# An adaLN, linear attention and SwiGLU block: shift and scale from eight row blocks of w_mod, and row tile 3 turned by a DMA

## The chip, the cores and the metric

The kernel runs on one core of a Trainium2 chip. The metric is the device time of one launch in microseconds. Eleven runs of the kernel before gave a median of 839.13 us (836.94 to 840.78).

## The reference

x is 2048 rows of 1024 features in bf16. A condition vector c gives six vectors of 1024: shift, scale and gate for the attention (sa, ca, ga) and for the feed-forward part (sb, cb, gb).

```
mod = silu(c) @ w_mod                      # 1024 x 6144 -> sa, ca, ga, sb, cb, gb
h = layernorm(x) * (1 + ca) + sa
q, k, v = split(h @ wqkv)                  # 32 heads of 32
pq, pk = phi(q), phi(k)                    # phi(t) = (t + 1 if t > 0 else exp(t)) + 1e-6
o = (pq @ (pk^T v)) / (pq @ sum(pk) + 1e-6)
x = x + ga * (o @ wo)
h = layernorm(x) * (1 + cb) + sb
x = x + gb * ((silu(h @ w_gate) * (h @ w_up)) @ w_down)
```

## The kernel before

The 2048 rows are four chunks of 512 (`sc`), each four row tiles of 128 (`t`). A normalised chunk is kept turned, features on partitions: `hT` is 128 partitions x 8 feature blocks (`cc`) x 512 rows. Shift and scale are then one value per partition and feature block, and `modulate` (line 217, instruction at 218) is one VectorE (DVE) operation for each `cc`. For every chunk come the keys (`k_mms`, 279: a group is one row tile and half of the columns, 8 matmuls over `cc`; eight groups, 64 matmuls), the values (`v_phase`, 297), and for the first chunk the queries; later the attention output and the feed-forward part follow.

This change is about the opening, up to the first value matmul. Both halves of `w_mod` that the attention needs (shift, columns 0 to 1023; scale, columns 1024 to 2047) are loaded here. Before, the view `wm_v` gives partition p the eight rows 8p to 8p + 7, and each tile `wme[b][q]` holds 512 columns of one of the two vectors, so rows of 1 KB are moved (`load_mod`, 130). SyncE's queue (SP) issues the loads in the order written in lines 123 to 149: x tiles 0 to 2, c, the first half of scale and of shift, key weights `wk` blocks 0 and 1 (`load_k`, 133), x tile 3, and so on; then the value weights `wv` (two tiles of 1 MB), x tiles 4 to 7 and the query weights `wq`.

`mod_block` (253) makes the columns of shift and scale: for each block of 128 columns eight matmuls with `w_mod` as stationary operand and the one column `scT` as moving one, so the result already lies on partitions. The layer norm of a tile is `ln1_stats` (231: two `bn_stats`, one aggregation on DVE, the power on GpSimd, POOL) and `ln1_norm` (238: ScalarE, ACT, or DVE for tile 3). In the first chunk TensorE turns the tiles (`pe_transpose_tile`, 221), and ACT and DVE share the copies out of PSUM. In later chunks a DMA turns them (`dma_start_transpose`, 245).

The order is written out by hand. `mm` and `transpose` (97 to 101) keep TensorE in program order, and the block `with in_order(...)` (424) does so for DVE, ACT and POOL. In it stand, on TensorE: tiles 0 to 2 turned, scale and shift of feature blocks 0 to 3, the first six key groups (row tiles 0 to 2) for `cc` 0 to 2, tile 3 turned, `cc` 3, then the second half's modulation between the rest. `keep_warm` (413) puts in filler matmuls whose result nobody reads: 20 at the start, 5 later. The tile framework gives each load from SP and ACT one of eight completion counters in turn; a load that takes a counter again waits until the load which used it last has landed.

Of the kernel before, what the change touches and what calls it, by code (L numbers as in the profile page):

```python
# [8 lines left out]
ACT = mybir.ActivationFunctionType  # L9
ALU = mybir.AluOpType  # L10
BF16 = mybir.dt.bfloat16
F32 = mybir.dt.float32
# [9 lines left out]
def kernel(  # L22
# [13 lines left out]
    nc = tc.nc  # L36
    P = nc.NUM_PARTITIONS
    _, S, D = A_x.shape
# [4 lines left out]
    DC = D // P  # L43
    HG = DC
    FC = F // P
    SCW = 512
    NSC = S // SCW
    STC = SCW // P
    NB = 512
# [13 lines left out]
    wg_v = B_w_gate.rearrange("(c p) f -> p c f", p=P)  # L63
    wu_v = B_w_up.rearrange("(c p) f -> p c f", p=P)
    wd_v = B_w_down.rearrange("(f p) n -> p f n", p=P)
    wm_v = w_mod.rearrange("(p j) n -> p j n", j=DC)
    c_v = c.rearrange("o (p j) -> p (o j)", j=DC)

    const = ctx.enter_context(tc.tile_pool(name="const", bufs=1))
    dram = ctx.enter_context(tc.tile_pool(name="dram", bufs=1, space=DRAM))  # L70
# [3 lines left out]
    ep = ctx.enter_context(tc.tile_pool(name="ep", bufs=3))  # L74
# [5 lines left out]
    last_on = {}  # L80
# [16 lines left out]
    def mm(out, lhsT, rhs, start, stop):  # L97
        return tc.keep_in_program_order(nc.tensor.matmul(out, lhsT=lhsT, rhs=rhs, start=start, stop=stop))  # L98

    def transpose(out, in_):  # L100
        return tc.keep_in_program_order(nc.tensor.transpose(out, in_, ident[:]))  # L101

    def big(name, shape):
        return k8.tile([P] + shape, BF16, name=name, tag="k8")
# [4 lines left out]
    def acc_b(name, shape=(NB,), dt=F32):  # L109
        return pb.tile([P] + list(shape), dt, name=name, tag="pb")  # L110

    x1_dram = dram.tile([S, D], F32, name="x1_scratch")

    c_sb = const.tile([P, DC], BF16, name="c_sb")

    x_tiles = {}

    def load_x(st, eng):
        x_sb = k2.tile([P, D], BF16, name="x_sb")
        eng.dma_start(out=x_sb[:], in_=x2[st * P:(st + 1) * P, :])  # L120
        x_tiles[st] = x_sb

    for st in range(STC - 1):
        load_x(st, nc.sync)
    nc.sync.dma_start(out=c_sb[:], in_=c_v)  # L125

    wk = [big("wk", [4, D]), big("wk", [4, D])]
    wme = [[big("wme", [DC, NB]) for _ in range(2)] for _ in range(2)]

    def load_mod(b, q, lo, hi):  # L130
        nc.sync.dma_start(out=wme[b][q][:, :, lo:hi], in_=wm_v[:, :, q * D + b * NB + lo:q * D + b * NB + hi])  # L131

    def load_k(cc):
        nc.sync.dma_start(out=wk[cc // 4][:, cc % 4, :], in_=wqkv_v[:, cc, D:2 * D])

    load_mod(0, 1, 0, NB)
    load_mod(0, 0, 0, NB)
    load_k(0)
    load_k(1)
    load_x(STC - 1, nc.sync)  # L140
    load_k(2)
    load_k(3)
    load_mod(1, 1, 0, NB)
    load_mod(1, 0, 0, NB // 2)
    load_k(4)
    load_k(5)
    load_mod(1, 0, NB // 2, NB)
    load_k(6)
    load_k(7)

    def load_w(view, lo, name):
        ts = []
# [11 lines left out]
    ident = const.tile([P, P], BF16, name="ident")  # L164
    make_identity(nc, ident[:])
    neg_half = const.tile([P, 1], F32, name="neg_half")
    nc.vector.memset(neg_half[:], -0.5)

    scT = const.tile([P, DC], BF16, name="scT")
    sc32 = const.tile([P, DC, 32], BF16, name="sc32")  # L170

    saT = const.tile([P, DC], F32, name="saT")
    ca1T = const.tile([P, DC], F32, name="ca1T")
    sbT = const.tile([P, DC], F32, name="sbT")
    cb1T = const.tile([P, DC], F32, name="cb1T")
    ga_t = ep.tile([P, NB], F32, name="e")
# [25 lines left out]
    def bn(src, mv_out):  # L202
        stats = small.tile([P, NNB, nc.vector.BN_STATS_DIM], F32, name="stats")
        for i in range(NNB):
            nc.vector.bn_stats(out=stats[:, i, :], in_=src[:, i * NB:(i + 1) * NB])
        nc.vector.bn_aggr(out=mv_out, in_=stats[:])

    def normalise(dst, src, mean, rstd):
        nc.vector.tensor_scalar(out=dst, in0=src, scalar1=mean, scalar2=rstd, op0=ALU.subtract, op1=ALU.mult)
# [7 lines left out]
    def modulate(hT, cc, scaleT, biasT, lo=0, hi=SCW):  # L217
        nc.vector.tensor_scalar(out=hT[:, cc, lo:hi], in0=hT[:, cc, lo:hi], scalar1=scaleT[:, cc:cc + 1],  # L218
                                scalar2=biasT[:, cc:cc + 1], op0=ALU.mult, op1=ALU.add)

    def pe_transpose_tile(hT, xn, t, split):
        tp = acc_b("tp", (DC, P), BF16)
        for cc in range(DC):
            transpose(tp[:, cc, :], xn[:, cc * P:(cc + 1) * P])
        if split < DC:
            nc.scalar.copy(out=hT[:, split:DC, t * P:(t + 1) * P], in_=tp[:, split:DC, :])
        nc.vector.tensor_copy(out=hT[:, 0:split, t * P:(t + 1) * P], in_=tp[:, 0:split, :])

    hTs = {}

    def ln1_stats(sc, t):
        x_sb = x_tiles.pop(sc * STC + t)
        mv = small.tile([P, STC, 2], F32, name="mv")
        bn(x_sb, mv[:, 0, :])
        rstd = rstd_of(mv, 1)
        return sc, t, x_sb, mv, rstd

    def ln1_norm(sc, t, x_sb, mv, rstd, dve=False):
        xn = k2.tile([P, D], BF16, name="xn", bufs=4)
        if dve:  # L240
            normalise(xn[:], x_sb[:], mv[:, 0, 0:1], rstd[:, 0:1])
        else:
            normalise_act(xn[:], x_sb[:], mv, rstd)
        if sc > 0:
            nc.sync.dma_start_transpose(hTs[sc][:, :, t * P:(t + 1) * P], xn[:])
        return xn
# [3 lines left out]
        for t in range(STC):  # L250
            ln1_norm(*ln1_stats(sc, t))

    def mod_block(b, q, lo, hi):
        for i in range(lo, hi):
            col = q * DC + 4 * b + i
            for j in range(DC):
                mm(mod_ps[:, col:col + 1], lhsT=wme[b][q][:, j, i * P:(i + 1) * P],
                   rhs=scT[:, j:j + 1], start=(j == 0), stop=(j == DC - 1))
        cs = slice(4 * b + lo, 4 * b + hi)
        src = mod_ps[:, q * DC + 4 * b + lo:q * DC + 4 * b + hi]  # L260
        if q == 1:
            nc.vector.tensor_scalar_add(out=ca1T[:, cs], in0=src, scalar1=1.0)
        else:
            nc.vector.tensor_copy(out=saT[:, cs], in_=src)

    last_phi = [None]

# [11 lines left out]
    def k_mms(sc, gs, accs, cc_lo=0, cc_hi=DC):  # L279
        for cc in range(cc_lo, cc_hi):  # L280
            for (t, nb), acc in zip(gs, accs):
                mm(acc[:], lhsT=hTs[sc][:, cc, t * P:(t + 1) * P], rhs=wk[cc // 4][:, cc % 4, nb * NB:(nb + 1) * NB],
                   start=(cc == 0), stop=(cc == DC - 1))
# [129 lines left out]
    def keep_warm(acc, n):  # L413
        for _ in range(n):
            mm(acc[:], lhsT=sel[:, 0, :], rhs=sel[:], start=True, stop=True)

    gs = k_groups[0:6]
    accs = [acc_a() if i < 4 else acc_b("acc") for i in range(6)]
    spare = accs[5]
    keep_warm(spare, 20)  # L420
    hT = hTs[0] = big("hT", [DC, SCW])
    pks[0] = big("pk", [STC, D])
    H = 3 * P
    with in_order(nc.vector, nc.scalar, nc.gpsimd):
        nc.scalar.activation(out=scT[:], in_=c_sb[:], func=ACT.Silu)
        xns = [ln1_norm(*ln1_stats(0, t)) for t in range(3)]
        mod_ps = acc_b("mod_ps")
        pe_transpose_tile(hT, xns[0], 0, DC)
        keep_warm(spare, 1)
        pe_transpose_tile(hT, xns[1], 1, DC)  # L430
        keep_warm(spare, 1)
        mod_block(0, 1, 0, 4)
        pe_transpose_tile(hT, xns[2], 2, DC // 2)
        keep_warm(spare, 3)
        for lo, hi in ((0, 1), (1, 4)):
            mod_block(0, 0, lo, hi)
            for cc in range(lo, hi):
                modulate(hT, cc, ca1T, saT, 0, H)
        k_mms(0, gs, accs, 0, 3)
        xn3 = ln1_norm(*ln1_stats(0, 3), dve=True)  # L440
        pe_transpose_tile(hT, xn3, 3, DC // 2)
        k_mms(0, gs, accs, 3, 4)
        for cc in range(4):
            modulate(hT, cc, ca1T, saT, H, SCW)
        mod_block(1, 1, 0, 4)
        gs7, accs7 = k_groups[6:7], [acc_b("acc")]
        k_mms(0, gs7, accs7, 0, 2)
        mod_block(1, 0, 0, 2)
        for cc in (4, 5):
            modulate(hT, cc, ca1T, saT)  # L450
        k_mms(0, gs7, accs7, 2, 4)
        k_mms(0, gs + gs7, accs + accs7, 4, 5)
        k_mms(0, gs[0:4], accs[0:4], 5, 6)
        mod_block(1, 0, 2, 4)
        for cc in (6, 7):
            modulate(hT, cc, ca1T, saT)
        k_mms(0, gs[4:6] + gs7, accs[4:6] + accs7, 5, 6)
        k_mms(0, gs + gs7, accs + accs7, 6, 8)
        gs8, accs8 = k_groups[7:8], [acc_b("acc")]
        k_mms(0, gs8, accs8)  # L460
        k_evac(0, gs, accs)
        k_evac(0, gs7, accs7)
        k_evac(0, gs8, accs8)
    with tc.issue_after(last_on[nc.vector.engine]):
        nc.vector.tensor_copy(out=sc32[:], in_=scT[:].unsqueeze(2).to_broadcast([P, DC, 32]))
    with tc.issue_after(last_on[nc.gpsimd.engine]):
        build_masks()

# [219 lines left out]
```

## Time and profile before

| | |
|---|---|
| median of 11 runs | 839.13 us |
| the profiled execution's own time | 840.0 us |
| its span | 838.0 us |
| first key matmul (chunk 0) starts | 15.13 us |
| first value matmul starts | 33.31 us |
| x tiles 0, 1, 2 landed | 3.43, 4.08, 5.35 us |
| first and second w_mod tile landed | 10.9, 13.9 us |
| first and second half of wv landed | 29.2, 31.9 us |
| a DMA that turns a tile, 28 of them, issue to landing | 3.0 to 8.9 us |

The profile is one execution. Its times count from the span's start. All matmuls show line 98 and all TensorE transposes line 101, the helpers that issue them, so groups are told apart by their tiles: `acc<-wk,hT` are keys, `acc<-wv,hT` values, `mod_ps` the modulation, `acc<-sel` the fillers. The landing of a DMA is its issue time plus the time to landing in the list of DMA issues; rates are the GB/s of a window.

### The profile page before, as it was taken

The numbers are of one execution on the slowest core, as the hardware profiler recorded it, in microseconds if no ns is written. First come the engines' busy times: TensorE is split into PE (matmuls) and PEld (weight loads), VectorE is DVE, ScalarE is ACT, GpSimd is POOL, SyncE is SP. The second block draws the span as 40 slices with busy tenths as digits, with TensorE's granted clock in tenths as the row PEclk, the third lists the DMA queues.
The fourth block names the chain that finished last, engine by engine and source line by source line (L and its number), as shares of the span: only waits on it lengthen the run. The fifth ranks groups of instructions, "written<-read, shape, count | busy, mean of one in ns | idle before, by whom it ended". The sixth has DMA issues, their size and how long they took to land.

```text
span 838.0 us, 11341 instructions
## 1 busy us (share of the span) xinstructions
PE 830.7 (99%) x4695; PEld 380.3 (45%) x4695; DVE 307.3 (37%) x597; ACT 169.9 (20%) x255; POOL 60.7 (7%) x165
## 2 busy tenths in 40 slices
PE   8999999999999999999999999999999999999998
PEld 3444444444444444444444444444444444444444
DVE  5656544487423324431111344222224431111122
ACT  2455353344211111101111010111110101111000
POOL 2011111112140001100000010000001100000000
PEclk9999999999999999999999999999999999999999
DMA  9894890029999446427434173581504539710011
GB/s 299 316 223 118 265 194 22 3 76 240 348 226 282 165 150 197 130 84 244 150 101 151 44 214 107 184 255 57 194 1 136 179 70 319 238 65 0 11 66 50
DMA packets 127795, 129.33 MB, mean 154 GB/s; under 512 B 34048, under 2 KB 109312, under 8 KB 127232
## 3 DMA queue, kind: packets, MB, share of 16 engines
q1 hardware_dynamic: 123696, 115.36, 46.5%
q0 software_dynamic: 4048, 13.25, 5.4%
q8 instruction: 36, 0.59, 0.3%
q14 instruction: 15, 0.12, 0.0%
HBM read 108.53 MB, written 12.72 MB: 145 GB/s over the span
## 4 chain that ended last, share of the span: by engine, by line
PE 98%; DMA 1%; DVE 0%; SPq 0%; issue 0%; ACT 0%
PE acc L98 89%; PE a_ps L98 7%; DMA wme<-in_w_mod_dram 1%; PE kvp L98 1%; PE modr L98 0%; PE mod_ps L98 0%; PE den L98 0%; SPq L120 0%; DVE wo L526 0%; PE wf L98 0%; DVE pq L273 0%; SPq L131 0%; ACT eb L270 0%; PE tp L101 0%; SPq L125 0%
## 5 line engine op out<-in xcount | busy, mean ns | idle before, releaser
L98 PE MATMUL acc<-h2T,wgu 128*128 128x512 bf16 x1792 | 387.6, 379 | 0.0
L98 PEld LDWEIGHTS <-wgu 128*128 128x128 bf16 x1792 | 175.1, 98 | 211.5
L98 PE MATMUL acc<-wd,gu 128*128 128x512 bf16 (+2 forms) x924 | 196.1, 373 | 0.0
L595 DVE TENSOR_TENSOR gu<-acc,e 128x512 bf16<-128x512 f32 x112 | 77.5, 692 | 299.3 <-PE acc L98 296.5
L594 ACT ACTIVATE e<-acc 128x512 f32<-128x512 f32 x112 | 66.9, 597 | 374.8 <-PE acc L98 374.8
L98 PEld LDWEIGHTS <-gu 128*128 128x128 bf16 x924 | 89.2, 98 | 104.5
L98 PEld LDWEIGHTS <-hT 128*128 128x128 bf16 x512 | 49.5, 98 | 61.2 <-issue 2.7
L616 DVE TENSOR_TENSOR e<-acc,gb_bc 128x512 f32<-128x512 f32 (+2 forms) x33 | 22.3, 675 | 129.8 <-PE acc L98 129.8
L98 PE MATMUL acc<-wk,hT 128*128 128x512 bf16 x256 | 59.5, 387 | 0.3 <-DVE hT L218 0.3
L98 PE MATMUL a_ps<-wo,pq 128*128 128x512 bf16 x256 | 57.4, 379 | 0.0
L98 PE MATMUL acc<-hT,wq 128*128 128x512 bf16 x256 | 56.8, 380 | 0.0
L98 PE MATMUL acc<-wv,hT 128*128 128x512 bf16 x256 | 55.9, 379 | 0.0
L270 ACT ACTIVATE eb<-acc 128x512 bf16<-128x512 f32 x64 | 37.9, 595 | 66.5 <-PE acc L98 63.4
L215 ACT ACTIVATE xn<-x,nmr,rstd 128x1024 bf16<-128x1024 f32 x16 | 19.8, 1240 | 126.3 <-POOL nmr L213 126.3
L563 POOL DMA_DIRECT2D x_scratch<-x x16 | 9.7, 608 | 418.5 <-DVE x L556 418.5
L98 PEld LDWEIGHTS <-pq 128*128 128x128 bf16 x256 | 25.0, 98 | 30.2
L98 PEld LDWEIGHTS <-wq 128*128 128x128 bf16 x256 | 24.5, 98 | 29.9 <-issue 0.9
L271 DVE TENSOR_SCALAR eb<-eb 128x512 bf16<-128x512 bf16 x64 | 18.5, 292 | 49.9 <-ACT eb L270 49.9
L556 DVE TENSOR_TENSOR x<-a_ps,x_sb 128x512 f32<-128x512 f32 x32 | 22.1, 691 | 7.9 <-PE a_ps L98 7.8
L199 POOL TENSOR_TENSOR rstd<-veps,neg_half 128x1 f32<-128x1 f32 x32 | 17.9, 559 | 75.5 <-DVE veps L197 73.2
L308 ACT CAST v<-acc 128x512 bf16<-128x512 f32 x32 | 18.2, 583 | 22.9 <-PE acc L98 22.9
L619 DVE TENSOR_TENSOR ob<-e,x1r 128x512 bf16<-128x512 f32 (+2 forms) x33 | 22.3, 675 | 1.0
(68 smaller groups left out, 261.5 us busy)
## 6 DMA issues: line engine op xcount, KB each, us to landing
wgu<-in_B_w_gate_dram SPq DMA_DIRECT2D x28, 1024.0 KB, 7.8
wgu<-in_B_w_up_dram SPq DMA_DIRECT2D x28, 1024.0 KB, 8.8
x_sb<-in_A_x_dram SPq DMA_DIRECT2D x32, 256.0 KB, 7.2
wml<-in_w_mod_dram SPq DMA_DIRECT2D x8, 1024.0 KB, 9.8
x_scratch<-x POOLq DMA_DIRECT2D x16, 512.0 KB, 3.5
x1r<-x_scratch SPq DMA_DIRECT2D x31, 256.0 KB, 3.0
wd<-in_B_w_down_dram SPq DMA_DIRECT2D x7, 1024.0 KB, 5.3
rbc<-rden_scratch POOLq DMA_DIRECT2D x16, 256.0 KB, 5.8
```

Source lines behind the costliest of these rows:

```text
L98: return tc.keep_in_program_order(nc.tensor.matmul(out, lhsT=lhsT, rhs=rhs, start=start, stop=stop))
L199: nc.gpsimd.tensor_tensor(out=rstd[:, 0:n], in0=veps[:, 0:n], in1=neg_half[:].to_broadcast([P, n]), op=ALU.pow)
L215: nc.scalar.activation(out=dst, in_=src, func=ACT.Identity, bias=nmr[:], scale=rstd[:, 0:1])
L270: nc.scalar.activation(out=e[:], in_=acc, func=ACT.Exp)
L271: nc.vector.tensor_scalar(out=e[:], in0=e[:], scalar1=1.0, scalar2=PHI_EPS, op0=ALU.min, op1=ALU.add)
L308: nc.scalar.copy(out=v[:, t * D + nb * NB:t * D + (nb + 1) * NB], in_=acc[:])
L556: nc.vector.tensor_tensor(out=x1[:, ns], in0=a_ps[:], in1=x_t[:, ns], op=ALU.add)
L563: nc.gpsimd.dma_start(out=x1_dram[st * P:(st + 1) * P, :], in_=x1[:])
L594: nc.scalar.activation(out=sg[:], in_=ps[0][:], func=ACT.Silu)
L595: gm = nc.vector.tensor_tensor(out=guT[sc][f // GPT][:, f % GPT, :], in0=ps[1][:], in1=sg[:], op=ALU.mult)
L616: nc.vector.tensor_tensor(out=yt, in0=y_ps, in1=gb_bc[:, ns], op=ALU.mult)
L619: nc.vector.tensor_tensor(out=ob, in0=yt, in1=x1r, op=ALU.add)
```

## The change

Partition p of `w_mod`'s view now has row p of each of eight blocks of 128 rows, and one load brings 2048 columns of one block: rows of 4 KB, 512 KB a load. The first of them, c and x tile 1 are issued from ACT, the others from SP; all eight come ahead of the key weights. c is loaded as 8 x 128 and turned by a matmul with the identity.

`mod_block(j)` now has the silu of c as stationary operand, repeated 32 times (`sc32`), and the block's rows as moving operand: four matmuls of 32 columns, one for each quarter of PSUM's partitions. The eight blocks add up in one bank; `mod_open` first writes 0 (shift) and 1 (scale) there. `mod_turn` brings the rows onto partitions with DVE's transpose of 32 x 32 squares: first for feature block 0, then for the other seven. There are 30 fillers, spread between the blocks.

The first six key groups run over `cc` 0 to 5 before tile 3's statistics are issued on DVE. Tile 3 is normalised by ACT and turned by a DMA issued from ACT; its eight shifts follow, then key groups 6 and 7 (tile 3) as wholes, after all other key groups.

```diff
-    wm_v = w_mod.rearrange("(p j) n -> p j n", j=DC)
+    wm_v = w_mod.rearrange("(j p) n -> p j n", p=P)
...
+    for j in range(DC):
+        (nc.scalar if j == 0 else nc.sync).dma_start(out=wme[j // 2][:, j % 2, :], in_=wm_v[:, j, 0:2 * D])
+    for cc in range(4):
+        load_k(cc)
     load_x(STC - 1, nc.sync)
+    for cc in range(4, DC):
+        load_k(cc)
...
+    def mod_open():
+        for g in range(4):
+            mm(mod_ps[32 * g:32 * g + 32, :], lhsT=ident[:, 0:32], rhs=base[:], start=True, stop=False)
+
+    def mod_block(j):
+        rows = wme[j // 2][:, j % 2, :].rearrange("p (n r) -> p n r", r=P)
+        for g in range(4):
+            mm(mod_ps[32 * g:32 * g + 32, :], lhsT=sc32[:, j, :], rhs=rows[:, :, 32 * g:32 * g + 32],
+               start=False, stop=(j == DC - 1))
+
+    def mod_turn(lo, hi):
+        src = mod_ps[:].rearrange("p (q i r) -> p q i r", q=2, r=32)
+        for q in range(2):
+            nc.vector.transpose(out=sca[:, q, lo:hi, :], in_=src[:, q, lo:hi, :])
...
-    keep_warm(spare, 20)
+    keep_warm(spare, 4)
...
+        c_ps = acc_b("mod_ps")
+        mm(c_ps[:, 0:DC], lhsT=c_sb[:], rhs=ident[0:DC, 0:DC], start=True, stop=True)
         mod_ps = acc_b("mod_ps")
+        mod_open()
+        nc.scalar.activation(out=scT[:], in_=c_ps[:, 0:DC], func=ACT.Silu)
+        st0 = ln1_stats(0, 0)
+        nc.vector.tensor_copy(out=sc32[:], in_=scT[:].unsqueeze(2).to_broadcast([P, DC, 32]))
+        xns = [ln1_norm(*st0)] + [ln1_norm(*ln1_stats(0, t)) for t in range(1, 3)]
...
+        turn(2)
+        mod_block(3)
+        for j, n in ((4, 3), (5, 4), (6, 4), (7, 4)):
+            keep_warm(spare, n)
+            mod_block(j)
+        keep_warm(spare, 4)
+        mod_turn(0, 1)
+        modulate(hT, 0, ca0T, sa0T, 0, P)
+        modulate(hT, 0, ca0T, sa0T, P, H)
+        mod_turn(1, DC)
+        for cc in range(1, DC):
+            modulate(hT, cc, ca0T, sa0T, 0, H)
+        nc.vector.tensor_copy(out=scaT[:], in_=sca[:, :, :, 0])
+        k_mms(0, gs, accs, 0, 6)
+        xn3 = ln1_norm(*ln1_stats(0, 3))
+        nc.scalar.dma_start_transpose(hT[:, :, H:SCW], xn3[:])
+        for cc in range(DC):
             modulate(hT, cc, ca1T, saT, H, SCW)
+        k_mms(0, gs, accs, 6, DC)
         gs7, accs7 = k_groups[6:7], [acc_b("acc")]
+        k_mms(0, gs7, accs7)
```

More of the change, by code (lines that the diff above doesn't have):

```diff
@@ L65 @@
     wd_v = B_w_down.rearrange("(f p) n -> p f n", p=P)
-    wm_v = w_mod.rearrange("(p j) n -> p j n", j=DC)
-    c_v = c.rearrange("o (p j) -> p (o j)", j=DC)
+    wm_v = w_mod.rearrange("(j p) n -> p j n", p=P)
+    c_v = c.rearrange("o (j p) -> (o j) p", p=P)
     const = ctx.enter_context(tc.tile_pool(name="const", bufs=1))
@@ L112 @@
     x1_dram = dram.tile([S, D], F32, name="x1_scratch")
-    c_sb = const.tile([P, DC], BF16, name="c_sb")
+    c_sb = const.tile([DC, P], BF16, name="c_sb")
     x_tiles = {}
@@ L121, in load_x @@
         x_tiles[st] = x_sb
-    for st in range(STC - 1):
-        load_x(st, nc.sync)
-    nc.sync.dma_start(out=c_sb[:], in_=c_v)
+    load_x(0, nc.sync)
+    load_x(1, nc.scalar)
+    load_x(2, nc.sync)
+    nc.scalar.dma_start(out=c_sb[:], in_=c_v)
     wk = [big("wk", [4, D]), big("wk", [4, D])]
-    wme = [[big("wme", [DC, NB]) for _ in range(2)] for _ in range(2)]
-    def load_mod(b, q, lo, hi):
-        nc.sync.dma_start(out=wme[b][q][:, :, lo:hi], in_=wm_v[:, :, q * D + b * NB + lo:q * D + b * NB + hi])
+    wme = [big("wme", [2, 2 * D]) for _ in range(DC // 2)]
     def load_k(cc):
         nc.sync.dma_start(out=wk[cc // 4][:, cc % 4, :], in_=wqkv_v[:, cc, D:2 * D])
[L136 to L139, printed above, removed]
+    for j in range(DC):
+        (nc.scalar if j == 0 else nc.sync).dma_start(out=wme[j // 2][:, j % 2, :], in_=wm_v[:, j, 0:2 * D])
+    for cc in range(4):
+        load_k(cc)
     load_x(STC - 1, nc.sync)
[L141 to L149, printed above, removed]
+    for cc in range(4, DC):
+        load_k(cc)
     def load_w(view, lo, name):
@@ L167 @@
     nc.vector.memset(neg_half[:], -0.5)
+    base = ep.tile([P, NB], BF16, name="eb")
+    nc.gpsimd.memset(base[:, 0:NB // 2], 0.0)
+    nc.gpsimd.memset(base[:, NB // 2:], 1.0)
     scT = const.tile([P, DC], BF16, name="scT")
     sc32 = const.tile([P, DC, 32], BF16, name="sc32")
-    saT = const.tile([P, DC], F32, name="saT")
-    ca1T = const.tile([P, DC], F32, name="ca1T")
+    scaT = const.tile([P, 2, DC], F32, name="scaT")
+    saT, ca1T = scaT[:, 0, :], scaT[:, 1, :]
+    sca_t = ep.tile([P, NB], F32, name="e")
+    sca = sca_t[:].rearrange("p (q i r) -> p q i r", q=2, r=32)
+    sa0T, ca0T = sca[:, 0, :, 0], sca[:, 1, :, 0]
     sbT = const.tile([P, DC], F32, name="sbT")
@@ L219, in modulate, with pe_transpose_tile @@
                                 scalar2=biasT[:, cc:cc + 1], op0=ALU.mult, op1=ALU.add)
-    def pe_transpose_tile(hT, xn, t, split):
+    def pe_transpose_tile(xn):
         tp = acc_b("tp", (DC, P), BF16)
@@ L224, in pe_transpose_tile @@
             transpose(tp[:, cc, :], xn[:, cc * P:(cc + 1) * P])
-        if split < DC:
-            nc.scalar.copy(out=hT[:, split:DC, t * P:(t + 1) * P], in_=tp[:, split:DC, :])
-        nc.vector.tensor_copy(out=hT[:, 0:split, t * P:(t + 1) * P], in_=tp[:, 0:split, :])
+        return tp
     hTs = {}
@@ L251, in ln1 @@
             ln1_norm(*ln1_stats(sc, t))
[L253 to L264, printed above, removed]
+    def mod_open():
[10 more added lines that the diff above has]
+            nc.vector.transpose(out=sca[:, q, lo:hi, :], in_=src[:, q, lo:hi, :])
     last_phi = [None]
@@ L424 @@
     with in_order(nc.vector, nc.scalar, nc.gpsimd):
-        nc.scalar.activation(out=scT[:], in_=c_sb[:], func=ACT.Silu)
-        xns = [ln1_norm(*ln1_stats(0, t)) for t in range(3)]
+        c_ps = acc_b("mod_ps")
+        mm(c_ps[:, 0:DC], lhsT=c_sb[:], rhs=ident[0:DC, 0:DC], start=True, stop=True)
         mod_ps = acc_b("mod_ps")
-        pe_transpose_tile(hT, xns[0], 0, DC)
-        keep_warm(spare, 1)
-        pe_transpose_tile(hT, xns[1], 1, DC)
-        keep_warm(spare, 1)
-        mod_block(0, 1, 0, 4)
@@ L433 @@
[L433 to L443, printed above, removed]
+        mod_open()
+        nc.scalar.activation(out=scT[:], in_=c_ps[:, 0:DC], func=ACT.Silu)
@@ new lines, with turn @@
+        st0 = ln1_stats(0, 0)
+        nc.vector.tensor_copy(out=sc32[:], in_=scT[:].unsqueeze(2).to_broadcast([P, DC, 32]))
+        xns = [ln1_norm(*st0)] + [ln1_norm(*ln1_stats(0, t)) for t in range(1, 3)]
+        def turn(t):
+            tp = pe_transpose_tile(xns[t])
+            nc.vector.tensor_copy(out=hT[:, :, t * P:(t + 1) * P], in_=tp[:])
+        keep_warm(spare, 2)
+        mod_block(0)
+        keep_warm(spare, 2)
+        turn(0)
+        mod_block(1)
+        keep_warm(spare, 2)
@@ new lines @@
+        turn(1)
+        mod_block(2)
+        keep_warm(spare, 1)
+        turn(2)
[11 more added lines that the diff above has]
+        nc.vector.tensor_copy(out=scaT[:], in_=sca[:, :, :, 0])
@@ L444 @@
+        k_mms(0, gs, accs, 0, 6)
+        xn3 = ln1_norm(*ln1_stats(0, 3))
+        nc.scalar.dma_start_transpose(hT[:, :, H:SCW], xn3[:])
+        for cc in range(DC):
             modulate(hT, cc, ca1T, saT, H, SCW)
-        mod_block(1, 1, 0, 4)
+        k_mms(0, gs, accs, 6, DC)
         gs7, accs7 = k_groups[6:7], [acc_b("acc")]
[L447 to L458, printed above, removed]
+        k_mms(0, gs7, accs7)
         gs8, accs8 = k_groups[7:8], [acc_b("acc")]
@@ L463 @@
         k_evac(0, gs8, accs8)
-    with tc.issue_after(last_on[nc.vector.engine]):
-        nc.vector.tensor_copy(out=sc32[:], in_=scT[:].unsqueeze(2).to_broadcast([P, DC, 32]))
     with tc.issue_after(last_on[nc.gpsimd.engine]):
```

## The prediction

> **What bounds the kernel now.** I read the page's busy table and the clock row first, then the chain of waits in order of time for 10 to 40 us, TensorE's own timeline there, the windows of 2 us, and last the landing times of single DMAs.
>
> The page:
> ```profile
> PE 830.7 (99%) x4695; PEld 380.3 (45%) x4695; DVE 307.3 (37%) x597; ACT 169.9 (20%) x255; POOL 60.7 (7%) x165
> PEclk9999999999999999999999999999999999999999
> ```
> TensorE is busy for 99% of the span; the fillers that keep it awake are in that. Nothing later has slack to take up a delay, so an edit to the opening is worth what it moves the first value matmul. Everything before that instant is judged by one number, which I call V.
>
> The chain in order of time, then TensorE's timeline:
> ```profile
> 3.30 10.59 DMA wme<-in_w_mod_dram
> ...
> 14.53 0.74 PE mod_ps L98 x24
> 15.27 5.59 PE acc L98 x18
> 20.86 0.45 PE tp L101 x8
> 21.31 1.29 PE acc L98 x6
> 22.61 0.78 PE mod_ps L98 x32
> ...
> 33.31 6.85 PE L98 MATMUL acc<-wv,hT 128*128 128x512 bf16 x31
> ```
> V is 33.31 us. Up to 13.88 the chain is the load of w_mod (wme). The first key matmul, T0, starts at 15.13. Six key matmuls in 1.29 us make 0.216 us each, so the 64 of the first row chunk need 13.8 us; they take 18.18. The 4.4 us between are 1.7 us of slow matmuls (18 in 5.59 us instead of 3.9), 2.0 us of modulation and transposes between them (0.45 + 0.78 + 0.39 + 0.38), and about 0.7 us of small waits.
>
> Windows of 2 us (the fields behind the engines are granted clock, DMA share, GB/s):
> ```profile
> 4.00:6.00 2.00, 2.00 (x6) 0.73 (x5) 1.93 (x6) 0.21 (x1) 0.61 (x2) 1.00 0.82 231
> 16.00:18.00 2.00, 2.00 (x7) 0.77 (x6) 1.93 (x6) 0.00 (x0) 0.00 (x0) 0.61 1.14 345
> 18.00:20.00 2.00, 2.00 (x6) 0.70 (x5) 0.64 (x2) 0.00 (x0) 1.70 (x26) 0.54 1.09 326
> 28.00:30.00 2.00, 1.97 (x10) 0.72 (x9) 0.78 (x3) 0.00 (x0) 0.00 (x0) 1.00 1.04 383
> ```
> The slow matmuls are a clock at about half (0.61, 0.54) right after a stretch in which TensorE mostly waited. The DMA engines are full throughout: 326 to 345 GB/s while 1 KB rows of w_mod are moved, 383 with 2 KB rows alone, and a slow 231 while the first w_mod tile starts.
>
> Single DMAs (KB each, us from issue to landing): a first tile of w_mod, the first half of wv, a turning DMA alone, and one beside another queue's store:
> ```profile
> wme<-in_w_mod_dram SPq DMA_DIRECT2D x1, 1024.0 KB, 8.3
> wv<-in_A_wqkv_dram SPq DMA_DIRECT2D x1, 1024.0 KB, 8.3
> hT<-xn SPq DMA_TRANSPOSE x1, 3.1
> x_scratch<-x POOLq DMA_DIRECT2D x1, 512.0 KB, 6.2
> h2T<-xn SPq DMA_TRANSPOSE x1, 6.6
> ```
> The same kind of turning DMA takes 3.1 us alone and 6.6 us (up to 8.9) when stores of another queue share the engines. That decides this forecast.
>
> **What the Trainium skill says.** "DMA: Bandwidth & Descriptors", Queues, rings and completion order: each DMA engine takes turns between the queues that have work. The trace agrees: between 190 and 192 us the turning moved 0.14 MB and the store 0.27 MB, 70 GB/s, where it moves about 210 GB/s alone. Same page, iDMA fabric: a load stream with 4 KiB rows ran at 408.7 GB/s alone; here no load has such rows, and wv with 2 KB rows lands at 388 (its halves land at 29.2 and 31.9). "TensorE: Matmul & The Clock Gate", Part 1: half clock after an idle window of about 3.4 us, full again after a busy one; the stretch from 16.4 to 19.7 us agrees. "TensorEngine Tiling (Array Packing)", Key Properties: column tiles run side by side; here 32 of the 32-column matmuls of mod_rows take 1.84 us, 0.23 per four.
>
> **The change, part by part.** t7 is the landing of the last w_mod block.
>
> *Rows of w_mod.* Before, half of shift and scale (2.1 MB) is enough for T0; now all 4.19 MB. x2 landed at 5.35. From there at 388 GB/s it is 10.8 us, plus about 0.5 for the start: t7 = 16.6. Bounds: at 408.7 GB/s without a start penalty 15.6; if the first block loses as much as the first tile did before (landed 5.5 us after x2, the next one 3.0 later: 2.5 us lost), 18.2 to 18.6. I take the low side because the slow start went with 1 KB rows: a lone 1 MB of wd with 2 KB rows lands in 5.3 us, of w_mod with 1 KB rows in 7.2 at least.
>
> *Behind t7.* Four 32-column matmuls 0.38 us to their end (cover for the other seven blocks: they and the 30 fillers, 0.216 each, run while DMA is waited for; uncovered, the fillers would be 6.5 us). mod_turn(0, 1), two small DVE transposes: no such row; 0.16 each like the DVE op on four columns, 0.36 with gaps. First shift on 128 columns 0.25, gaps 0.15. So T0 = t7 + 1.2 = 17.8, 2.7 later than before. The matmul that turns c and mod_open's four are hidden likewise (uncovered 0.23 each).
>
> *Taken off the key phase.* The second half's modulation, the eight transposes and the small waits go (2.7 us), and, if the fillers keep the clock up, the 1.7. The second key block waits for the big mod_turn: 128x224 is bounded by 0.16 and 0.69 us (four columns, 512 columns of f32 from PSUM), I take 0.39 twice, so DVE needs 0.33 + 0.78 + 0.32 = 1.4 against six matmuls of 1.3: 0.2 lost. The 48 matmuls of tiles 0 to 2 end at t7 + 1.2 + 10.35 + 0.2 = t7 + 11.75. Were nothing late, V = t7 + 15.2 = 31.8.
>
> *Row tile 3.* The first tile-3 matmul waits for this chain. DVE is through with seven shifts (7 x 0.32) and the copy at t7 + 4.8; statistics 1.65 (rows 205, 206, 197), POOL 0.55 + 0.27 and gaps 1.0, ACT's normalise 1.24 (row 215): t7 + 8.75. The x tile itself lands by t7 + 3.4 (four key blocks and itself, 1.31 MB at 388), in time. Besides, in the built program's instruction list the turning DMA on ACT waits for the completion counter that the first half of wv used. That half is issued when k1 has landed (t7 + 1.35), with k2 to k7 and x3 ahead (1.83 MB, 4.7 us) and its own 2.7: t7 + 8.75 too. So the turning is issued at t7 + 8.85, whichever is taken away. Queued behind it on ACT: the Exp table load (1.28) and the Exps of the evacuation, which are due only at t7 + 11.5: free. On DVE the eight shifts of tile 3 stand ahead of all key evacuations.
>
> *The turning's latency L.* Alone 3.0 to 3.6. But here wv's second half, x4 to x7 and wq, 4.2 MB, are on SP's queue at that moment, 10.8 us of DMA work. Worked out: 1.2 to first data (issued 188.26, data from 189.45), 256 KB at 70 GB/s 3.7, and 0.6 to the semaphore (as x0: data through at 2.85, landed 3.43): 5.5. Seen: 6.6 to 8.9. I take 6.5; ends 3.0 and 8.9.
>
> *Behind it.* Gap 0.1, eight shifts of 0.245 as seven key matmuls follow one by one, last matmul 0.27, then the eighth group 1.73: 4.05. V = t7 + 8.85 + L + 4.05 = t7 + L + 12.9 = 36.0. TensorE stands still for about 4 us before tile 3: t7 + 15.7 against t7 + 11.75. The accumulators of the values are free by then: the first two key evacuations (0.95 each on DVE) follow the shifts at t7 + 17.4, V is t7 + 19.4.
>
> *The rest.* sc32 moves ahead of the second statistics, 0.28 on DVE, early, hidden by the wait for w_mod (uncovered 0.28). Two POOL memsets and three DMA issues on ACT (about 0.4 each) run in the first 3 us, beside the table load; SP's queue gets as many bytes as before. Masks on POOL move behind tile 3's rstd, needed far later. Nothing.
>
> **Sum.** 36.0 - 33.3 = +2.7 us. The profiled execution took 840.0 (span 838.0); the median of the runs is 0.9 lower, 839.13. Forecast 839.1 + 2.7 = 841.8.
>
> **The rivals.** (1) *Faster: the opening is DMA-bound and tile 3 is in time enough.* With t7 = 15.6 and L = 3.0, V = 31.5, 1.8 earlier: 837.3. It decides at t7 + L below 18.7; no change lies at 20.4, a loss of 0.2% at 22.1, my values give 23.1. For it: the full DMA rates, and the 4.4 us that the key phase sheds. Against it: turning beside another queue's traffic never took under 6.6 us. In the middle between, t7 = 16.6 and L = 4, V is 33.5: no change, 839.3. (2) *The standstill drops the clock.* About 4 us without matmuls before tile 3 may bring the half clock as 13 to 16.4 us did before: 3.4 us at half, 1.7 lost, 843.5. Against: the idle time may straddle two windows. (3) *w_mod late or first keys at half clock.* The start penalty stays (t7 18.4) or the fillers don't suffice: +1.7 to 1.8, 843.6. Against: fillers and fours make 1.1 of each 1.35 us busy.
>
> **How the numbers follow.** The plain standstill 0.45 (0.36 slower, 0.09 same); with the clock drop 0.20; late w_mod or slow keys 0.12; in time 0.23 (0.15 same, 0.08 faster). Faster 0.08, same 0.24, slower 0.68, with 0.2% (1.7 us) about what a measurement of this kernel can tell from no change. Range: from t7 + L = 20.1 (V 33.0, 838.8), in rival 1, to t7 + L = 24.6 with the clock drop (+4.2 and +1.7, 845.0); past the two ends I leave some 0.1 each.
>
> **What would show it.** Right: a TensorE wait of 2 to 5 us on the DVE shift of hT, itself on the turning DMA, ahead of the last sixteen key matmuls; T0 near 17.8; clock 1.00 after T0; V near 36. Wrong: the turning landing in under 4.5 us beside the wv and wq loads, t7 past 18 or before 16, or a clock of 0.5 in the first keys.

## The result, and the profile after

The changed kernel takes 850.1 us (median of 8 runs, 849.24 to 850.87), the kernel before beside it 838.92 (31 runs): a ratio of 1.0134, 95% interval 1.0122 to 1.0147. The forecast was 841.8, range 838.8 to 845.0. The direction and the place were right; the loss, 11.2 us, is four times the 2.7 that I forecast. The profiled execution has a span of 848.9 us against 838.0.

The page of the changed kernel:

```profile
PE 833.4 (98%) x4601; PEld 378.6 (45%) x4601; DVE 307.5 (36%) x599; ACT 170.4 (20%) x254; POOL 61.6 (7%) x168
PEclk9799999999999999999999999999999999999999
```

TensorE is now busy for 98%, and the second slice of 21 us (21 to 42 us) has a lower clock. The chain in order of time for the first 60 us (start, length, what):

```profile
1.74 6.78 DMA wme<-in_w_mod_dram
...
8.56 0.62 PE mod_ps L98 x4
...
17.96 0.97 PE acc L98 x4
18.93 0.36 PE mod_ps L98 x4
...
25.74 1.25 ACT xn L212
26.99 0.02 issue
27.02 9.98 DMA hT<-xn
...
37.39 22.72 PE acc L98 x92
```

Between 8.56 and 19.29 us the chain never leaves TensorE: blocks, turns and fillers one after the other, no load of w_mod among them. Then DVE, POOL and ACT make row tile 3, and the turning DMA stands in the chain for 9.98 us. TensorE's timeline has the price (in brackets its idle time and what ended it), and the windows show the clock (behind the five engines: granted clock, DMA share, GB/s):

```profile
20.07 10.52 PE L98 MATMUL acc<-wk,hT 128*128 128x512 bf16 x48
37.39 6.32 PE L98 MATMUL acc<-wk,hT 128*128 128x512 bf16 x16 [6.81 <-DVE hT L215]
43.55 13.98 PE L98 MATMUL acc<-wv,hT 128*128 128x512 bf16 x64
```
```profile
12.00:14.00 2.00, 2.00 (x27) 1.22 (x25) 0.71 (x2) 0.00 (x0) 0.00 (x0) 1.00 1.02 412
32.00:34.00 2.00, 0.00 (x0) 0.00 (x0) 0.00 (x0) 0.00 (x0) 0.00 (x0) 0.66 1.09 391
38.00:40.00 2.00, 2.00 (x6) 0.66 (x5) 1.97 (x8) 0.08 (x1) 0.00 (x0) 0.50 0.00 0
```

TensorE stood still for 6.81 us and ran the 16 key matmuls of tile 3 at half clock, in 6.2 instead of 3.5 us. V, the first value matmul, is 43.55 where I had 36.0 and the kernel before 33.31. The 7.55 us, term by term:

| term | forecast | measured | off by |
|---|---|---|---|
| first key matmul T0 | 17.8 | 20.07 | +2.3 |
| T0 to the issue of the turning DMA | 7.65 | 6.95 | -0.7 |
| turning DMA, issue to landing (L) | 6.5 | 10.0 | +3.5 |
| landing to first value matmul | 4.05 | 6.55 | +2.5 |

From V to the end of the span it is 805.35 us, 804.7 before. Of the other 0.66, 0.5 is a pause of TensorE in the second group of mod_rows (2.41 instead of 1.91 us).

### The profile page after: what moved, and what is told of

The parts are those of the page before. It is cut to its first block, busy times and chain, and to the rows that moved or that the text cites. A ratio compares the mean times of both kernels' runs of the same rounds, so it can differ in the third digit from the quotient of the medians.

```text
span 848.9 us, 11170 instructions
## 1 busy us (share of the span) xinstructions
PE 833.4 (98%) x4601; PEld 378.6 (45%) x4601; DVE 307.5 (36%) x599; ACT 170.4 (20%) x254; POOL 61.6 (7%) x168
## 4 chain that ended last, share of the span: by engine, by line
PE 96%; DMA 2%; DVE 1%; ACT 0%; ACTq 0%; POOL 0%; issue 0%
PE acc L98 88%; PE a_ps L98 7%; DMA hT<-xn 1%; DMA wme<-in_w_mod_dram 1%; PE kvp L98 1%; PE modr L98 0%; PE mod_ps L98 0%; DVE hT L215 0%; PE den L98 0%; PE tp L101 0%; ACT xn L212 0%; DVE wo L530 0%; DVE stats L202 0%; PE wf L98 0%; DVE e L261 0%
## 5 line engine op out<-in xcount | busy, mean ns | idle before, releaser
L98 PEld LDWEIGHTS <-wq 128*128 128x128 bf16 x256 | 24.6, 98 | 29.8 <-issue 0.9
L212 ACT ACTIVATE xn<-x_sb,nmr,rstd 128x1024 bf16<-128x1024 bf16 x16 | 19.8, 1240 | 23.8 <-POOL nmr L210 23.7
```

Source lines behind the costliest of these rows:

```text
L212: nc.scalar.activation(out=dst, in_=src, func=ACT.Identity, bias=nmr[:], scale=rstd[:, 0:1])
```

## The experiments

My theory after the result was the "backlog theory": ACT's queue gets nearly nothing until SP's queue is through, so the turning lands with the end of the query weights (the last of those landed near 36 us, the turning at 37.0). Rivals: sharing has a fixed price of about 10 us; or the late first keys are what costs. The times of the kernel before beside the runs were 839.2 to 839.5. "First keys", "V" and "block 0" below are from each kernel's profile.

**1. TensorE turns tile 3** (e1_pe_turn)

```diff
-        nc.scalar.dma_start_transpose(hT[:, :, H:SCW], xn3[:])
+        tp3 = pe_transpose_tile(xn3)
+        nc.vector.tensor_copy(out=hT[:, :, H:SCW], in_=tp3[:])
```

> Row tile 3 is turned by TensorE and copied by DVE instead of the DMA from ACT; all else as in the changed kernel. Backlog theory (the turning DMA waits for SP's queue to drain, and the standstill also halves the clock): no standstill, tile 3 turned at about 28, first value matmul near 34.5 instead of 43.55, so 841 us (9.0 less than 850.1). Rival (the late first keys are what costs, 2.3 us beyond the forecast, and the DMA only fills a wait that is there anyway): 848 to 850.

Measured: 843.6 (ratio to before 1.0056, 1.0037 to 1.0076), 6.5 less than the change. No standstill, clock 1.00, V 35.45. So the DMA costs the larger part, as the theory had it. But 2 us are missing. 0.9 is block 0, at 9.44 here (8.56 in the profile of the change). The rest stands 95 us later, in TensorE's timeline:

```profile
128.80 1.24 PE L98 MATMUL acc<-wk,hT 128*128 128x512 bf16 x5
131.91 1.25 PE L98 MATMUL acc<-wk,hT 128*128 128x512 bf16 x5 [1.87 <-issue]
```

TensorE waited 1.87 us, and the profile shows no releaser. In the DMA view of 129 to 131 us one packet of an instruction queue (0.02 MB) is moved, just as the long loads of wo end. I come back to it under 8.

**2. Nineteen fillers left out, the DMA kept** (e2_no_late_fill)

```diff
-        for j, n in ((4, 3), (5, 4), (6, 4), (7, 4)):
+        for j, n in ((4, 0), (5, 0), (6, 0), (7, 0)):
...
-        keep_warm(spare, 4)
         mod_turn(0, 1)
```

> The 19 fillers behind row block 3 are left out. First keys 20.07 to about 16.8. Backlog theory: the turning DMA is issued earlier (about 25) but lands when SP's queue is through, 36 to 37 as before, so 849.5 to 850.5: the earlier keys gain nothing. Rival with a fixed price for sharing (10 us from issue to landing whatever the queue holds): landing at 35, about 848. Rival that late keys are what costs: 3.3 us less, 846.8.

Measured: 847.9 (1.0115, 1.0089 to 1.0142). First keys at 17.18, 2.9 earlier. The turning is issued at 25.16, 1.9 earlier, and its data are used by DVE from 35.88, 1.1 earlier:

```profile
35.88 1.87 DVE L215 TENSOR_SCALAR hT<-hT,scaT 128x128 bf16<-128x128 bf16 x8 [14.02 <-DMA hT<-xn]
```

Issue to landing is 10.7 us. Here it was the counter of wv's first half that let the turning go: that load landed at 25.08. The time is what the fixed price gives, but partly by luck: 1.2 of the 2.2 us come from the key matmuls of tile 3, of which less fell into half clock (5.1 us instead of 6.3). The landing, 35.9, lies between the fixed price's 35 and the backlog theory's 36 to 37. The DMA view of 31 to 32 us in this kernel decides more (queue: packets, MB, share of 16 engines; q1 is SP's, q10 ACT's):

```profile
DMA packets 358, 0.39 MB, mean 392 GB/s; under 512 B 189, under 2 KB 189, under 8 KB 358
...
q1 hardware_dynamic: 177, 0.35, 89.2%
q10 hardware_dynamic: 181, 0.05, 20.4%
```

The turning gets its packets while SP's queue is still full, as many as SP's: against the backlog theory. The rate of the changed kernel from 33 to 34 us, in 40 slices of 25 ns, shows the turns themselves:

```profile
GB/s 31 1106 338 0 236 1075 164 0 287 1106 82 20 532 922 0 20 1116 338 0 133 942 410 0 276 1034 164 10 369 1024 82 20 799 604 82 92 584 748 82 62 533
```

A burst comes about every four slices, and the first four slices hold 36.9 KB, just what 16 engines move if each takes one packet of 2 KB and one of 256 B. So the engines take one packet of each queue in turn, and ACT's queue has half of the packets and an eighth of SP's bytes: 0.045 MB a us. By that the 1024 packets of the turning need 1024 / 177 = 5.8 us, an estimate that e2 bears out: they were moved from 29.2 to 35.2 us. The first of them was moved only some 4 us after the issue. 4 + 6 and the signal make the 10.7 us of e2.

The 10.0 us of the change are made up a little differently. The first packet came at 31.0, again 4 us after the issue. Then SP's queue ran out (130 of its packets from 34 to 35 us, against 432 of the turning), so nearly all were through by 35.3, some 4.3 us later. A few stragglers, up to 36.5, and the signal took the remaining 1.7.

**3. The query weights held back** (e3_wq_later: loaded behind a two-element write of ACT that follows the turning's issue), and the same with the fillers left out (e10_wq_no_fill)

```diff
-    wq = load_w(wqkv_v, 0, "wq")
...
         nc.scalar.dma_start_transpose(hT[:, :, H:SCW], xn3[:])
+        wq = [big("wq", [4, D]) for _ in range(2)]
+        for h in range(2):
+            nc.scalar.copy(out=wq[h][:, 0, 0:1], in_=xn3[:, 0:1])
+            nc.sync.dma_start(out=wq[h][:], in_=wqkv_v[:, 4 * h:4 * h + 4, 0:D])
```

> The two loads of the query weights (2 MB) are issued only after ACT has issued the turning DMA. Backlog theory: only x tiles 4 to 7 stand ahead at 27 us, the turning lands at 30.5 to 32 (3.5 to 5 us), first value matmul at 35 to 36, 841.5 to 842.5. Rival with a fixed price for sharing: 8 to 10 us to landing while any load shares the engines, 847 to 850.

> The DMA from ACT turns row tile 3, with the query weights held back until it is issued and the late fillers left out. Backlog theory: issued at 25 behind the value weights' counter, landing in 5 to 6 us at 30 to 31, first value matmul at 34 to 35: 840.3 to 841.5, some 2 us more than with TensorE's turn and the fillers left out (839.0), the price of the DMA without a backlog. Rival (the DMA costs the same 10 us again): 846 or more.

Measured: 843.75 (1.0058, 1.0036 to 1.0079) and 848.6 (1.0112, 1.0096 to 1.0128). From the DMA issues, first e3, then e10 (KB, us to landing):

```profile
hT<-xn ACTq DMA_TRANSPOSE x1, 5.0
```
```profile
hT<-xn ACTq DMA_TRANSPOSE x1, 10.6
```

In e3 the query weights were issued at 28.87, as the x tiles ran out. SP's queue was nearly empty from 30 to 31 us, with 19 packets against 303 of the turning, and L was 5.0. The time lies 1.3 us above the range that I expected. In e10 everything is 2.8 us earlier while the x tiles are not, and the query weights joined at 26.2. The turning landed at 35.0, before the query weights (37.1 and later): against the backlog theory once more. L was 10.6 again, the rival's number, but no full queue made it. The DMA view of e10 from 30 to 31 us:

```profile
DMA packets 230, 0.13 MB, mean 126 GB/s; under 512 B 192, under 2 KB 192, under 8 KB 230
...
q10 hardware_dynamic: 189, 0.05, 95.8%
q1 hardware_dynamic: 41, 0.08, 43.7%
```

SP's queue moves 41 packets here and not some 180, and the 189 of the turning take 95.8% of the engines' time, where 181 took 20.4% in e2. From 30 to 34 us both queues together moved 126 to 184 GB/s. Packets in turn don't explain that, and neither does any run here; the cause stays open.

**4. Query weights in rows of 1 KB** (e13_wq_1k, to test packets in turn)

```diff
-    wq = load_w(wqkv_v, 0, "wq")
+    wq = [big("wq", [4, D]) for _ in range(2)]
+    for h in range(2):
+        for lo in range(0, D, 512):
+            nc.sync.dma_start(out=wq[h][:, :, lo:lo + 512], in_=wqkv_v[:, 4 * h:4 * h + 4, lo:lo + 512])
```

> The query weights come in four loads with rows of 1 KB instead of two with 2 KB; the turning DMA from ACT beside them is unchanged, but its counter is now that of x tile 4, so it is issued at about 28.2 instead of 27.0. Packet theory (the engines alternate between the queues one packet for one, 256 B of turning against one row of the load; about 4 us until the first packet): each round is shorter with 1 KB rows, 64 rounds of about 57 ns are 3.6 us instead of 5.8, so 7.5 to 8.5 us from issue to landing. Backlog theory (the turning is through when SP's queue is): landing at 36 to 37, so 8 to 9 us as well but with SP's queue ending then. Fixed price: 10 to 10.7 us, landing at 38.5. The number of packets of each queue in the windows before the landing tells them apart.

Measured: 850.9 (1.0138, 1.0122 to 1.0154); L is 8.9 us, landing at 37.15. The DMA view of 33 to 34 us:

```profile
q1 hardware_dynamic: 280, 0.28, 80.0%
q10 hardware_dynamic: 287, 0.07, 32.3%
```

One for one again, now 287 instead of 181 packets of the turning a us: 1024 / 287 = 3.6 us, and about 4.3 us until the first packet. L itself decides nothing: 8.9 lies just above what packets in turn gave (7.5 to 8.5) and within what the backlog theory gave (8 to 9). The counts are what speaks for packets in turn: they followed the row size. The whole time shows no gain, since the turning was issued 1.25 us later (its counter was that of x tile 4). Why the first packet takes 4 us here, about 2 in e3 and 1.2 alone, no run settled.

**5. The turning issued from SP, and block 0 from SP** (e5_sp_turn, e6_w0_sp)

```diff
-        nc.scalar.dma_start_transpose(hT[:, :, H:SCW], xn3[:])
+        nc.sync.dma_start_transpose(hT[:, :, H:SCW], xn3[:])
```
```diff
-        (nc.scalar if j == 0 else nc.sync).dma_start(out=wme[j // 2][:, j % 2, :], in_=wm_v[:, j, 0:2 * D])
+        nc.sync.dma_start(out=wme[j // 2][:, j % 2, :], in_=wm_v[:, j, 0:2 * D])
```

> The DMA that turns row tile 3 is issued from SP, behind the query weights in the same queue, instead of from ACT. Backlog theory (a second queue gives the turning almost nothing while SP's queue is full): it lands within 1 us of where ACT's did, 36 to 38, and the time stays at 849 to 851. Rival (the engines do take turns, ACT's queue wins it several us): it lands at 40 or later, 853 or more.

> The first w_mod block is issued from SP instead of ACT. If the two queues sharing the engines is what made it land at 8.5 to 9.4 us, after the second block, it lands at 6.5 to 7.2 now, and the first keys come at about 18.5 instead of 20.1. Since the turning DMA lands with the end of SP's queue, that gains little: 849 to 850. Rival (late first keys cost what they are late): 848.5 or less.

Measured: 850.2 (1.0132, 1.0112 to 1.0152) and 850.3 (1.0129, 1.0106 to 1.0152), both as the change. For e5 the backlog theory had expected just this, so that run alone doesn't speak against it. A place at the end of SP's queue (L 8.9, landing 37.1) is worth as much as a queue of ACT's own. Block 0 from SP came at 7.62, not at 6.5 to 7.2, and the first keys at 19.53, with L again 10.5.

**6. Fillers in the standstill** (e4_fill_stall)

```diff
+        keep_warm(accs7[0], 28)
         k_mms(0, gs7, accs7)
```

> 28 filler matmuls (6.05 us) stand between the first six key groups and those of tile 3, so that TensorE does not idle. If the half clock is what made the 16 matmuls take 6.2 instead of 3.5 us: 2.7 us less, 847.4, clock 1.00 from 31 to 44 us. Rival (the eight shifts on DVE pace them): no change, 850.

Measured: 849.8 (1.0130, 1.0110 to 1.0152). TensorE's timeline:

```profile
31.03 6.21 PE L98 MATMUL acc<-sel 128*128 128x512 bf16 x28
38.46 3.67 PE L98 MATMUL acc<-wk,hT 128*128 128x512 bf16 x16 [1.22 <-DVE hT L215]
...
52.74 1.89 PE L98 MATMUL acc<-wv,hT 128*128 128x512 bf16 x8 [0.25 <-ACT v L305]
55.48 1.89 PE L98 MATMUL acc<-wv,hT 128*128 128x512 bf16 x8 [0.85 <-ACT v L305]
```

The clock stayed at 1.00 and the 16 matmuls took 3.5 us, so it was the clock and not DVE that stretched them. But the time hardly moved. The key evacuations stand behind the shifts of tile 3 on DVE, behind those the statistics of the next chunk, and behind its normalising ACT's copies of the values, for which TensorE now waits. Counted from the first shift of tile 3 to the first query matmul it is 19.1 us here (38.09 to 57.21) and 20.3 in the change (37.02 to 57.36): 1.2 of the 2.7 us remain, the rest goes to the next wait. The landing was 1.1 later in this profile.

**7. TensorE turns tile 3, and fewer fillers** (e7_pe_turn_no_fill: edits 1 and 2; e9_no_fill_w0: block 0 from SP as well; e14_some_fill: as e9, with 1, 2, 2, 2 and 2 of the late fillers; e8_best: as e9, with all but five of the late fillers and nine more ahead of block 0)

> Row tile 3 turned by TensorE, and the 19 late fillers left out. Without the DMA the first keys set the end, so leaving the fillers out is now worth what it moves them, 3 us less what a half clock in the first keys costs (0 to 1.7): 840.5 to 842.5, where the same edit with the DMA was worth 2.2. Rival (the fillers are hidden behind the loads): 843.6 as with them.

> Row tile 3 turned by TensorE, late fillers left out, and the first w_mod block from SP. The chain starts about 1.5 to 2 us earlier (first block at 7.6 instead of 9.6), so the last block's landing near 15.5 to 16.4 sets the first keys: 16.7 to 17.5 instead of 18.1. 0.6 to 1.4 us less than without the third edit: 837.6 to 838.4. Rival (half clock in the first keys, or the wait for instructions, takes it back): 839 to 840.5.

> Row tile 3 turned by TensorE, the first w_mod block from SP, nine late fillers (1, 2, 2, 2 and 2 behind the last block) instead of 19 or none. If they keep the clock up and no wait for instructions falls into 125 to 132 us: first keys at 17.3 to 17.9, first value matmul at 31.6 to 32.2, 837.5 to 838.3, below the kernel before. If half clock returns in the first keys: 839 to 839.5. If the wait for instructions returns: 839 to 840.5.

> Row tile 3 turned by TensorE, the first w_mod block from SP, nine more fillers ahead of the first block (in the wait for it) and five fewer behind. Chain from the first block at about 7, clock full from there: first keys at 16.8 to 17.5, first value matmul at 31.3 to 32.2: 1.1 to 2.0 us below the kernel before, 837 to 838.5. Rival (TensorE waits for its instructions later, as the profile with the turned tile showed once for 1.9 us): 839 to 840.5.

| kernel | median | ratio to before, interval | block 0 | first keys | V |
|---|---|---|---|---|---|
| e7 | 839.0 | 0.9995, 0.9985 to 1.0004 | 9.65 | 18.12 | 32.39 |
| e9 | 839.4 | 1.0005, 0.9996 to 1.0014 | 7.88 | 17.97 | 33.92 |
| e14 | 839.0 | 0.9997, 0.9988 to 1.0005 | 7.41 | 17.50 | 31.77 |
| e8 | 840.45 | 1.0012, 1.0005 to 1.0019 | 7.95 | 18.09 | 32.34 |

e7 lands 1.5 us below its expectation. The same edit of fillers was worth 2.2 us with the DMA and 4.6 without it (3.1 of them in the first keys, 1.9 the wait under 1 that isn't there). The fillers were not hidden behind the loads. e9 shows what they are for, in its windows:

```profile
18.00:20.00 2.00, 1.78 (x5) 0.74 (x7) 1.96 (x8) 0.00 (x0) 0.00 (x0) 0.53 1.06 407
20.00:22.00 2.00, 2.00 (x7) 0.75 (x6) 2.00 (x7) 0.00 (x0) 0.00 (x0) 0.61 1.06 403
```

Half clock in the first keys, 36 matmuls in 9.5 instead of 7.8 us: its rival's case. e7 has no late fillers either and keeps its clock (1.00 from 18 to 22 us): with block 0 at 9.65 TensorE had work without a gap up to 16.5. e14, with nine fillers, keeps the clock too and has V 1.5 us below the kernel before; the median of its 14 runs is 0.5 below, which the interval doesn't tell from no change. e8 has as good a V and loses 1.3 us to a wait of TensorE at 127.4, of the kind seen under 1. None of them beats the kernel before by more than the measurement can tell.

**8. wo held back** (e11_wo_later: e1 with the loads of wo behind the second modulation row, and DVE's scaling of wo behind the last values; e12_best_wo_later: e9 with the same)

```diff
+                row = mod_rows(blks)
+                mod_spread(sc - 2, row)
+            if sc == 3:
+                wo = [big("wo", [4, D]) for _ in range(2)]
+                for h in range(2):
+                    for i in range(4):
+                        nc.scalar.copy(out=wo[h][:, i, 0:1], in_=row[:, 0:1])
```

> Row tile 3 turned by TensorE with all fillers (843.6 before, 1.9 us of it a wait of TensorE for instructions near 131 us), and the loads of wo, which filled the DMA queue then, held back until the second modulation row is out. If the instruction fetch waited behind those loads, that wait goes: 841.5 to 842. Rival (the wait belongs to the program's layout): 843.6.

> As the kernel with TensorE's turn, no late fillers and the first block from SP, with wo held back as well. No wait for instructions above 0.5 us: 837.4 to 838.2, 1.2 to 2 us below the kernel before. Rival (the wait moves elsewhere or half clock in the first keys takes it): 839 or more.

Measured: 849.3 (1.0121, 1.0105 to 1.0137) and 844.6 (1.0065, 1.0051 to 1.0080), both far off. The longest waits of TensorE and of DVE in e11:

```profile
PE acc L98 <- DVE pk L270: 3.9, 1, 3.9
```
```profile
DVE sbT L365 <- DMA mcol<-mrow_scratch: 7.9, 1, 7.9
```

The second modulation row takes a way over DRAM: POOL issues stores of 1 KB, then a load of 4 KB (`mcol`). Now the loads of wo fill SP's queue just then. In e1 such a store landed in about 1.6 us and the load in 4.7; in e11 the last store took 5.6 and the load 6.1. DVE waited 7.9 us for the load (2.4 in e1), a key evacuation stood behind that, and TensorE waited 3.9 us for it and then ran at half clock (0.50 from 150 to 155 us). In e12 it was 8.0 and 4.0 us. So holding back wo moved it beside other small transfers on the path, and these paid.

On the question itself the pair says little. In e11 the wait without a releaser is gone (0.2 us at most), but in e7, e9 and e14 it is gone too, with wo where it was, so e12 had nothing to gain there. That TensorE waits for instructions behind the loads of wo is not shown; the cause stays open.

## Why the prediction was right or wrong

**What held.** The bookkeeping by V: from there to the end both kernels take 805 us. (It is no law: in e4 V came 1.6 us earlier and the time fell by 0.3.) The load of w_mod: the windows move 403 to 422 GB/s with rows of 4 KB, as the 408.7 of the Trainium skill ("DMA: Bandwidth & Descriptors", iDMA fabric) said. Rows of 2 KB moved 404 to 414 from 27 to 30 us too, so the row size need not be the reason. t7 was about 15.3 (the last block was issued at 5.2 and took 10.1), 1.3 earlier than I took and below my lowest, 15.6; t7 before 16 was one of my signs of being wrong. The key phase: 48 matmuls in 10.52 us (10.55). The DVE transposes: 0.16 and 0.36 us each (0.16 and 0.39). The chain of tile 3 from T0: 6.95 (7.65). The counter of wv's first half wasn't what held the turning: that load landed at 24.9, ACT was ready at 26.99. It would have been next (e2: 25.08). The place of the loss: TensorE's wait for the turned tile.

**T0, the step "Behind t7 ... cover".** I put T0 at t7 + 1.2, with blocks and fillers hidden under the loads. They weren't. Block 0, issued from ACT in rivalry with SP's queue, landed only at 8.5, and then the work left for TensorE, 20 of the fillers, three turns and eight blocks (0.33 us each, not 0.23), at half speed at first (0.49 us a filler, then 0.24), filled all the time to 19.29. TensorE, not DMA, set T0: it came 4.8 us behind t7, not 1.2. The table's +2.3 is small by luck, since t7 was 1.3 early. I had even written the price of the failed cover, 6.5 us, and put it into no bound. Leaving out 19 fillers moved T0 by 2.9 (e2) and 3.1 (e1 to e7).

**L, the step "The turning's latency".** The mechanism was right, engines that take turns, and the term was mis-sized: 6.5, measured 10.0. The largest part is the first packet: it came after 4 us instead of 1.2, and no run explains that. Then the rate: I took 70 GB/s from a case in which the other queue was a store that had only 66 packets, of 4 KB, to 542 of the turning. Against a full queue the turns are one packet for one: 45 GB/s with 2 KB rows, about 6 us in e2 instead of 3.7. In the change SP's queue ran out earlier, so that it was 4.3 us and then stragglers: 1.7 to the landing, where I had 0.6 for the signal. The 8.9 that I gave as upper end was only the longest that the trace happened to hold. The Trainium skill's page "DMA: Bandwidth & Descriptors", Queues, rings and completion order, gives a whole packet of several descriptors as the unit of a turn; here the 256 B and 2 KB pieces, as the trace counts them, alternate singly (36.9 KB in four slices of 25 ns), and the measurement decides.

**What follows the landing, the step "Behind it", and rival 2.** With 6.8 us of standstill the half clock came, which I held for a case of 0.20; it made 2.5 us of this term where I had priced 1.7. In the end it was worth about 1.2 (e4), since the evacuations on DVE were late anyway.

**The range.** Its upper end did join a longer L with the clock drop: t7 + L = 24.6 (measured 25.3) and 1.7 us. What it had nowhere is a T0 set by TensorE, 3.6 us more; with the 0.8 us by which the half clock was dearer, that is what put V past 39.2, its upper end, to 43.55. That e7, without the DMA and without the 19 fillers, is back at 839.0 shows that these two hold the whole loss.

## What to carry to other kernels

A DMA with small packets beside a busy queue is to be priced by packets in turn, not by its bytes: its packets times the time of one turn, and some us more until its first packet. (One kernel here, e10, was slow in another way.) A transfer that TensorE waits for is better kept off a moment when bulk loads fill the engines, or done on another engine: 0.45 us of TensorE and a copy on DVE took the place of 10 us of DMA here. Moving the bulk loads instead can put them beside another small transfer (e11). Fillers count as hidden only if the first real data come early enough; look whether the chain of waits leaves TensorE at all.

## What the runs showed of the hardware that I had not expected

- A DMA transpose beside a queue of 2 KB rows: 10.0 to 10.7 us in four kernels, 8.9 beside 1 KB rows, 5.0 where the queue ran dry, 3.0 to 3.6 alone. Two queues got 177 and 181 packets in the same us, with 2 KB and 256 B each.
- In e10 it took 10.6 us while both queues together moved only 126 to 184 GB/s for 4 us; unexplained.
- Stores of 1 KB and a load of 4 KB took 5.6 and 6.1 us beside the loads of wo (e11), 1.6 and 4.7 without (e1).
- A half-megabyte load issued from ACT at 1.74 landed at 8.5 (up to 9.7 in other runs), after one that SP had issued at 1.64 (7.5). From SP the first block landed at 7.4 to 7.9.
- Four matmuls on column tiles with a moving operand of 32-element pieces took 0.33 us, 0.23 with a contiguous one.
- TensorE stood 0.4 to 1.9 us without a releaser near 126 to 139 us in several kernels, and not in others whose instructions differ by a few fillers.
